# One pool of eight PSUM banks, a fourth output buffer, later loads on SyncE alone, and a new order for an attention and ELU-MLP kernel

## The chip, the cores and the metric

The kernel runs on one core of one Trainium2 chip. The metric is the device time of one execution in microseconds, as a median over runs. Engines: TensorE (PE) for matmuls, VectorE (DVE), ScalarE (ACT), GpSimd (POOL), and SyncE (SP), which only issues DMAs here; ScalarE and GpSimd issue some as well.

## The reference

Causal attention with 16 extra "beacon" keys and values that every query sees, over 8 batches and 8 heads of 576 tokens with 64 columns, and then a two-layer MLP with an ELU between, over all 4608 tokens.

```python
k_all = concatenate([beacon_k, k], axis=2)        # 16 + 576 keys
v_all = concatenate([beacon_v, v], axis=2)
scores = q @ k_all^T / 8, causal on the 576 own keys
a = exp(scores - max) / (sum + 1e-9)
x = (a @ v_all) reshaped to [B * S, H * D] = [4608, 512]
h = x @ w_in                                       # 512 -> 2048
out = where(h > 0, h, exp(min(h, 0)) - 1) @ w_out  # 2048 -> 512
```

All inputs and the output are float32.

## The kernel before

**The work.** A batch is taken as four pairs of heads (n = 4 * batch + pair). For batches 0 to 2 (below `PE_B`) queries and keys of a pair are loaded into an `st` buffer, cast into an `sb` buffer and transposed on TensorE (`do_T`, `do_T2`); from batch 3 on they are loaded by tokens (`load_tok`, `load_tok2`), cast (`cast_tok`) and transposed by SP as DMA transposes (`turn_tok`, line 446, ten for a batch). Values go through `vst` buffers (`load_v`, `cast_v`). Scores are computed in units (`do_SC`, line 504): the matmuls of a unit use 64 rows of TensorE for each of the two heads and fill two PSUM banks. ScalarE takes the exponential of a unit (`do_exp`, line 513) into an `et` buffer, GpSimd masks it (`do_mask`, line 518), TensorE multiplies with the values and a column of ones (`do_AV`, line 532), and VectorE divides (`do_norm`, lines 545 and 546). The result is transposed into `xT`, a ring of four batches: on TensorE for batches 0 and 1 (`do_xT`), and as DMA transposes on SP from batch 2 on (`turn_x`, line 552).

**The MLP** runs over eleven tiles of tokens (128, 128, 256, then 512 each). `do_mm1` (line 584) makes one bank of 512 columns from four matmuls; ScalarE takes its exponential (`do_e`, line 591), GpSimd clamps that (`do_clamp`, line 595), VectorE joins both into `gt` (`do_join`, line 602), and then the bank is free. `do_mm2` (line 626) adds up sixteen matmuls, in four steps, in one bank for 128 tokens; VectorE copies it to an `osb` buffer (`do_osb`, line 632) and SP stores it (`do_store`, line 636). A `fill` (line 334) is a matmul on a column of ones without use for the result; it keeps TensorE at work while it would wait.

**The order.** Nothing runs in the order in which it is written. `Program.add` gathers 1734 operations, each with the engines that may take it, what it depends on, and which buffers it takes and gives back. `Program.run` then goes through the list `ORDER` (numbers of operations; -k stands for k fills), with `PICKS` naming the engine of each operation that has a choice and `PLACES` the number of each buffer. Each engine runs its own operations in this order, and waits where an input or a buffer is not ready. The lists come from a planner that is not part of the kernel.

**PSUM** is eight banks of 512 float32. Before, four of them are single banks ("bank": `do_mm1`, `do_mm2`, `do_AV`, `do_xT`, `do_T2`, fills) and four form two pairs ("pair": `do_SC`, `do_T`). Three `osb` buffers, six `st` and six `vst` buffers are on hand. Loads may be issued by SP or by ScalarE ("SA"); 27 load operations are ScalarE's, eight of them for batch 0 and the rest spread up to batch 7.

Of the kernel before, what the change touches and what calls it, by code (L numbers as in the profile page):

```python
# [8 lines left out]
FP32 = mybir.dt.float32  # L9
# [4 lines left out]
P = 128  # L14

ORDER = [i for t in """
# [96 lines left out]
class Program:  # L113
# [7 lines left out]
    def run(self, order, picks, places, fill):  # L121
# [10 lines left out]
        for i in order:  # L132
# [5 lines left out]
            op = self.ops[i]  # L138
            assert not op.done and all(d.done for d in op.deps)
            got = []  # L140
            for room in op.take:
                at = int(next(places), 36)
                assert (room, at) not in used
                used.add((room, at))
                op.held.append((room, at))
                got.append(self.rooms[room][at])
# [743 lines left out]
```

## Time and profile before

| | |
|---|---|
| median of 3 runs | 350.59 us (349.97 to 351.15) |
| the profiled execution | 349.6 us, of which its span is 347.8 us |
| granted TensorE clock, mean | 0.999 |
| moved by DMA | 52.54 MB, 127664 of 140631 packets under 512 B |
| DMA engines' busy share | 0.7 to 0.9 in most slices up to 260 us, near 0 in several after that |

The profile is of one execution. Times are in microseconds from the start of the span; "PE bank L584 x8" is eight TensorE instructions of line 584 that write a tile named bank. Matmuls overlap, so the time between two starts, not the length of one, says what it costs. SPq and ACTq are the DMA-issuing instructions of SP and ScalarE. The waits give, for an engine that stood idle, what ended that; the chain follows the work that ended last back from the end.

### The profile page before, as it was taken

The page shows a single profiled execution, that of the slowest core. Times are in us where ns is not written, and L with a number is a line of the kernel's source. Part 1 is how long each engine was busy: PE and PEld are TensorE (multiplying, and loading weights), DVE is VectorE, ACT ScalarE, POOL GpSimd, SP SyncE. Part 2 cuts the span into 40 slices and gives each one's busy share as a digit, 9 for nine tenths or more (in the row PEclk, how much of TensorE's full clock was granted, in tenths as well). Part 3 has the DMA queues.
Part 4 walks back from the last instruction along what each step waited for, and adds up shares of the span by engine and source line. Part 5 has one row for each costly group of instructions (what it writes and reads, how often), then busy time and mean ns, then how long its engine had stood idle before and what let it go on. Part 6 is the DMA issues. An engine that isn't in the chain of part 4 may idle for free.

```text
span 347.8 us, 8391 instructions
## 1 busy us (share of the span) xinstructions
PE 337.6 (97%) x3300; PEld 192.2 (55%) x3300; DVE 184.0 (53%) x399; ACT 203.7 (59%) x296; POOL 190.3 (55%) x357
## 2 busy tenths in 40 slices
PE   7999999999998999999999999999999999999996
PEld 5667787454553555455466764456445554444444
DVE  4777685465541665366335552656255634744431
ACT  1786795678717891796477455886197504632300
POOL 2687897457545676566358643765085503642400
PEclk9999999999999999999999999999999999999999
DMA  7999999899799999997899699955740062000112
GB/s 211 236 243 237 188 221 228 200 268 153 161 211 142 191 208 175 186 177 170 142 224 218 136 190 210 158 96 121 122 111 2 5 181 76 0 14 18 60 61 92
DMA packets 140631, 52.54 MB, mean 151 GB/s; under 512 B 127664, under 2 KB 134064, under 8 KB 140592
## 3 DMA queue, kind: packets, MB, share of 16 engines
q1 hardware_dynamic: 115264, 41.78, 58.4%
q10 hardware_dynamic: 21104, 6.03, 8.7%
q0 software_dynamic: 4224, 4.19, 7.5%
q8 instruction: 26, 0.43, 0.6%
q14 instruction: 13, 0.11, 0.1%
HBM read 37.22 MB, written 9.44 MB: 134 GB/s over the span
## 4 chain that ended last, share of the span: by engine, by line
PE 86%; DMA 6%; DVE 2%; issue 1%; POOL 1%; SPq 1%; ACT 1%; ACTq 0%; POOLq 0%; DVEq 0%
PE bank L626 35%; PE bank L584 34%; PE bank L532 8%; PE pair L504 8%; DMA w_in<-in_moe_w_in_dram 3%; DMA out_dram<-osb 2%; DMA st<-in_q_dram 1%; PE pair L386 1%; PE bank L334 1%; SPq L365 1%; ACT et L513 1%; POOL et L518 0%; DVE x L546 0%; PE bank L561 0%; DVE sb L331 0%
## 5 line engine op out<-in xcount | busy, mean ns | idle before, releaser
L513 ACT ACTIVATE et<-pair 128x1024 f16<-128x1024 f32 (+3 forms) x113 | 103.5, 957 | 64.6 <-PE pair L504 60.1
L584 PE MATMUL bank<-xT,w_in 128*128 128x512 f16 (+2 forms) x768 | 134.9, 326 | 2.6 <-DMA w_in<-in_moe_w_in_dram 1.3
L626 PE MATMUL bank<-w_out,gt 128*128 128x512 f16 (+1 forms) x592 | 133.8, 373 | 0.0
L602 DVE SCALAR_TENSOR_TENSOR gt<-e,bank 128x512 f16<-128x512 f32 x144 | 95.9, 685 | 68.8 <-POOL e L595 67.9
L595 POOL TENSOR_SCALAR e<-e 128x512 f32<-128x512 f32 x144 | 87.3, 612 | 74.6 <-ACT e L591 73.3
L591 ACT ACTIVATE e<-bank 128x512 f32<-128x512 f32 x144 | 84.5, 604 | 57.9 <-PE bank L584 56.4
L584 PEld LDWEIGHTS <-w_in 128*128 128x128 f16 x768 | 66.9, 98 | 56.0 <-issue 4.2
L518 POOL TENSOR_SCALAR_AFFINE_SELECT et<-et 128x256 f16<-128x256 f16 (+3 forms) x145 | 59.1, 424 | 54.4 <-ACT et L513 54.1
L626 PEld LDWEIGHTS <-gt 128*128 128x128 f16 x592 | 55.4, 98 | 59.6 <-issue 1.3
L632 DVE COPY osb<-bank 128x512 f32<-128x512 f32 (+1 forms) x37 | 24.8, 674 | 55.9 <-PE bank L626 43.4
L532 PEld LDWEIGHTS <-et 128*128 128x128 f16 (+1 forms) x960 | 34.8, 97 | 8.4 <-issue 1.0
L532 PE MATMUL bank<-v,et 128*128 128x65 f16 (+1 forms) x960 | 37.2, 193 | 0.3 <-DVE x L546 0.3
L504 PE MATMUL pair<-qT,kT 64*128 64x80 bf16 (+4 forms) x744 | 35.3, 225 | 1.1 <-ACT et L513 1.1
L546 DVE TENSOR_TENSOR x<-bank,rl 128x256 f16<-128x256 f32 (+2 forms) x68 | 32.1, 472 | 2.3
L331 POOL CAST sb<-st 128x1024 bf16<-128x1024 f32 (+4 forms) x30 | 28.2, 940 | 8.0 <-DMA st<-in_q_dram 8.0
L504 PEld LDWEIGHTS <-kT 64*128 64x128 bf16 x744 | 20.9, 95 | 19.1 <-issue 15.6
L545 DVE RECIPROCAL rl<-bank 128x4 f32<-128x4 f32 (+2 forms) x68 | 12.4, 182 | 21.2 <-PE bank L532 20.7
L334 PE MATMUL bank<-ones 128*128 128x256 bf16 x76 | 14.4, 311 | 1.3 <-DVE ones L841 1.3
L331 POOL CAST v<-vst 128x512 f16<-128x512 f32 (+1 forms) x20 | 12.2, 617 | 3.2 <-DMA vst<-in_v_dram 2.0
L329 ACT ACTIVATE v<-vst 128x512 f16<-128x512 f32 (+1 forms) x19 | 11.4, 632 | 0.0
L334 PEld LDWEIGHTS <-ones 128*128 128x128 bf16 x76 | 7.6, 110 | 4.5 <-issue 1.4
L329 ACT ACTIVATE sb<-st 128x1024 bf16<-128x1024 f32 (+3 forms) x10 | 9.4, 948 | 0.0
(39 smaller groups left out, 68.7 us busy)
## 6 DMA issues: line engine op xcount, KB each, us to landing
out_dram<-osb SPq DMA_DIRECT2D x35, 256.0 KB, 2.7
vst<-in_v_dram SPq DMA_DIRECT2D x18, 256.0 KB, 4.6
st<-in_q_dram SPq DMA_DIRECT2D x15, 256.0 KB, 5.1
st<-in_k_dram SPq DMA_DIRECT2D x12, 256.0 KB, 4.5
st<-in_k_dram SPq DMA_DIRECT2D x8, 288.0 KB, 5.6
st<-in_q_dram SPq DMA_DIRECT2D x8, 288.0 KB, 7.1
w_in<-in_moe_w_in_dram POOLq DMA_DIRECT2D x4, 512.0 KB, 10.5
w_out<-in_moe_w_out_dram POOLq DMA_DIRECT2D x4, 512.0 KB, 9.1
```

The source lines that it names most:

```text
L331: e.tensor_copy(out=out, in_=in_)
L334: nc.tensor.matmul(out=bank[:, 0:2 * P], lhsT=ones[:, 0:P], rhs=ones, start=True, stop=True)
L504: e.matmul(out=pair[:, h, o:o + w], lhsT=kT[D * h:D * h + D, P * jc:P * jc + P], rhs=qT[D * h:D * h + D, q0:q0 + w], start=True, stop=True ...
L513: e.activation(out=et[:, :, 0:w], in_=scs[n, u][:, :, 0:w], func=AFT.Exp, bias=0.0, scale=float(1.0 / (D ** 0.5)))
L518: e.affine_select(out=part, in_=part, compare_op=ALU.is_ge, fill=fill0, base=q0 + NB - P * jc, pattern=[[0, 2], [0, times], [1, dw]], chan ...
L532: e.matmul(out=av[:, c:c + D + 1], lhsT=ets[tuple(unit)][0:m, h, col:col + P], rhs=v16s[b % 2][0:m, jc, 2 * hp + h, 0:D + 1], start=(jc == ...
L546: e.tensor_tensor(out=x16s[b % 2][:, blks[0]:blks[-1] + 1:step, P * hp:P * hp + P].rearrange("q i (h d) -> q i h d", d=D), in0=av[:, :, :, ...
L584: e.matmul(out=bank[:, o:o + z - a], lhsT=w_in16[:, cc, P * fc:P * fc + P], rhs=xTa[:, cc, a % RING:a % RING + z - a], start=(cc == 0), st ...
L591: e.activation(out=t, in_=hpss[p, i], func=AFT.Exp, bias=0.0, scale=1.0)
L595: e.tensor_scalar(out=t, in0=t, scalar1=1.0, scalar2=0.0, op0=ALU.min, op1=ALU.max)
L602: e.scalar_tensor_tensor(out=gts[p, i // 2][:, i % 2], in0=es[p, i], scalar=1.0, in1=hpss[p, i], op0=ALU.subtract, op1=ALU.max)
L626: e.matmul(out=opss[p, t4][:, cols], lhsT=gt_of(p, fc)[:, P * t4:P * (t4 + 1)], rhs=w_out16[:, fc, cols], start=(fc == 0), stop=(fc == NFC ...
```

## The change

All eight banks lie in four tiles of two banks. A "bank" is one half of such a tile, a "pair" is the whole, so that any single bank may be taken by any of the single-bank operations, and up to four pairs may be in use at once. The bookkeeping of `Program.run` counts a pair as its two banks. There is a fourth `osb` buffer. Values of batches from `PE_B` = 3 on and all token loads (`load_tok`, `load_tok2`) are issued by SP alone ("S"); the loads of batches 0 to 2 may still be ScalarE's. `ORDER`, `PICKS` and `PLACES` are new in whole, planned with SP's own pace. ScalarE now has 6 load operations (four for batch 0, two for batch 2); fills are 78 instead of 76.

```diff
             for room in op.take:
                 at = int(next(places), 36)
-                assert (room, at) not in used
-                used.add((room, at))
-                op.held.append((room, at))
+                held = [("bank", at), ("bank", at + 1)] if room == "pair" else [(room, at)]
+                assert not used.intersection(held) and not (room == "pair" and at % 2)
+                used.update(held)
+                op.held.append(held)
...
             for other, i in op.give:
-                used.remove(other.held[i])
+                assert used.issuperset(other.held[i])
+                used.difference_update(other.held[i])
...
+    pairs = [psum.tile([P, 2, 512], FP32, name=f"banks_{i}") for i in range(4)]
...
-        "osb": tiles(3, [P, DM], FP32, "osb"),
-        "bank": [psum.tile([P, 512], FP32, name=f"bank_{i}") for i in range(4)],
-        "pair": [psum.tile([P, 2, 512], FP32, name=f"pair_{i}") for i in range(2)],
+        "osb": tiles(4, [P, DM], FP32, "osb"),
+        "bank": [pairs[i // 2][:, i % 2] for i in range(8)],
+        "pair": [pairs[i // 2] for i in range(8)],
...
-            got = add("SA", load_v, b, jc, take=["vst"])
+            got = add("SA" if b < PE_B else "S", load_v, b, jc, take=["vst"])
...
-                st = add("SA", load_tok, b, is_k, c, take=["st"])
-                got = [st] + ([add("SA", load_tok2, b, is_k, c + 1, deps=[st])] if m == 2 else [])
+                st = add("S", load_tok, b, is_k, c, take=["st"])
+                got = [st] + ([add("S", load_tok2, b, is_k, c + 1, deps=[st])] if m == 2 else [])
...
```

The three lists `ORDER`, `PICKS` and `PLACES` are left out here.

More of the change, by code (lines that the diff above doesn't have):

```diff
@@ L16 @@
 ORDER = [i for t in """
[69 rows of a table removed]
[69 rows of a table added]
 """.split() for i in ([int(t)] if int(t) >= 0 else [-1] * -int(t))]
 PICKS = (
-    "GSVAGSGSGSGSAVVSSGVASVVSSVAAAVVAAGVASVVSSVVVVAVVVVVVAVAASASASASGSGSSGASSGVSSGVSSGVVVAVGSAAASAAASGSSGASSAASSGVS"
-    "SGVSGSGAASASGSSASSGSGSSASSGSGSGSAAGSGSGSSGSSGAGSSGASGSAAASGSGSASGASGSAGSAASASSASGSASAAASGAASAGSSASGASGSSGSGAAS"
-    "GSASASGAAGSSASASAGASGSG"
+    "GSVAGSGSASGSAVVSSVVASVVSSGVSSGVSSGVASVVSSVVVVAVAVVVAVAVASASASASGSGSSGASSGVSSGVSSGVAAVVGSGAGSGSGSGSSGASSGVSAAVS"
+    "SGVAAAGGGGGGGGGGGGAGGGAAGAGAGAGGAGGAAGGAAGGAAGGAGAAGGAAGGA"
@@ L91 @@
 )
 PLACES = (
-    "00101111111111111111111012213333333333212300233333333331101322222111003214215333306333033312011113127010003123"
-    "31105741135400120221121630203001123130120301231332451000111102323215070011112323300010121421522106223330001361"
-    "1452273050173310100132210563113100320301112323203042351201418041712950330A22101323B101120C2021001211D321320006"
-    "100033E0135431200211312F20010310012111014071120022101030152340000113025172021100312131G150320H1062131003043221"
-    "20704132214201503302110110623301310371223001204623120214013020311203421151701032110301252515060233E1F101405003"
@@ L98 @@
-    "202317001191203213201200322B033C101022D0110617300101210511230318A350212430135012230313H1221340043131G201230012"
-    "2100130201227301061137500031423111201231054204250711000021031221203160312103112039220132C1112236100107122303F1"
-    "2015015203031001B13123104202110031210321D3E0612102000133A0711052102301G31041511120301232012014011803H123211003"
-    "213600302001102147335122C112300322611130032211300322B1130900F1303211108222033213000G210E2301112132H00321130011"
-    "200111320"
+    "01001111111111111111111101111111131111223211114111106014220233034652222000000040627655542111111100323150622443"
@@ new lines @@
+    "33500020046471121615323423137603224536725505435521400655440216210100477732300131243516211324001252665124226337"
+    "037063220745304640207136254531646016345010467440672400153210465031207810292A304350B7610111323C04521202242501D2"
+    "432E16205053060143206003641F3765320420415603275250601244051037601321140251621004460672112634420260G7143H550601"
+    "421063711013422040321103327260160432511704203564512614060210655130324602113020264572064202400312135261E5127533"
+    "41F012B022426553423067044261D3012A251403C226074022003562140656732120891001021036011601252541431H71030246141322"
@@ L103 @@
+    "00230G5645316004212360543112270273607100034230112422041405641502032723301710B0012E405231225A502103721D23603122"
+    "7046076213165044262003124200132614025345043C12F61G730220314H10461007234230361526321104610473012242706451902071"
+    "464512033154736162801B7063242D2710021135E2305A20143601222737043521214201073423C21F15090011326G0274015013223411"
+    "70212170302"
 )
```

138 rows, old and new, of the table ORDER are left out of this document.

## The prediction

> **What bounds the kernel now.** I read the page first (span, busy shares, the chain that ended last), then the busy time by stretches, then the waits, and last the timeline around each place where TensorE stood still.
>
> ```profile
> span 347.8 us, 8391 instructions
> PE 337.6 (97%) x3300; PEld 192.2 (55%) x3300; DVE 184.0 (53%) x399; ACT 203.7 (59%) x296; POOL 190.3 (55%) x357
> PE 86%; DMA 6%; DVE 2%; issue 1%; POOL 1%; SPq 1%; ACT 1%; ACTq 0%; POOLq 0%; DVEq 0%
> ```
>
> TensorE is busy 97% of the span and is 86% of the chain; no other engine passes 59%. The only time to win is TensorE's own work and the 347.8 - 337.6 = 10.2 us in which it idles. The busy time by stretches (first column the window, then its length, then TensorE's busy time) says where those lie:
>
> ```profile
> 0.00:40.00 40.00, 35.33 (x492) 26.62 (x492) 26.48 (x94) 24.29 (x36) 26.47 (x55) 1.00 1.02 229
> 40.00:105.00 65.00, 64.98 (x744) 39.20 (x741) 39.16 (x83) 44.11 (x66) 42.93 (x80) 1.00 1.01 203
> 105.00:115.00 10.00, 8.74 (x79) 4.06 (x79) 2.55 (x5) 6.92 (x10) 5.10 (x10) 1.00 1.01 153
> 115.00:170.00 55.00, 55.00 (x590) 29.13 (x587) 31.95 (x65) 39.24 (x56) 36.02 (x68) 1.00 0.98 183
> 170.00:175.00 5.00, 3.91 (x42) 1.86 (x35) 0.00 (x0) 2.60 (x3) 0.80 (x2) 1.00 0.94 118
> 175.00:340.00 165.00, 165.00 (x1338) 87.86 (x1337) 82.39 (x150) 86.54 (x128) 79.02 (x144) 1.00 0.51 106
> 340.00:347.80 7.80, 4.67 (x38) 3.47 (x36) 1.45 (x3) 0.00 (x0) 0.00 (x0) 0.97 0.20 70
> ```
>
> Idle: 4.7 us in the start, 1.3 around 110, 1.1 around 173, 3.1 at the end, nothing elsewhere; the granted clock is 1.00 throughout. So an edit can gain in the middle only by ending those two stops (2.4 us) or by making TensorE's own instruction stream shorter.
>
> **The stream itself: changes between score and other matmuls.** The scores (L504) use 64 rows, all else in the middle of the kernel uses 128 (or 80). From the timeline of TensorE (start, length, what) and the chain:
>
> ```profile
> 158.59 1.03 PE L626 MATMUL bank<-w_out,gt 128*128 128x512 f16 x4
> 159.55 0.39 PE L504 MATMUL pair<-qT,kT 64*128 64x256 bf16 x4
> 159.88 0.54 PE L532 MATMUL bank<-v,et 128*128 128x65 f16 x12
> ...
> 120.72 0.61 PE L504 MATMUL pair<-qT,kT 64*128 64x256 bf16 x8
> 121.26 0.71 PE L532 MATMUL bank<-v,et 128*128 128x65 f16 x18
> ...
> 242.49 7.77 PE bank L626 x36
> ```
>
> A 512-column matmul in an unbroken stream takes 7.77 / 36 = 0.216 us. The four before the scores at 159.55 took 159.55 - 158.59 = 0.96 instead of 0.86: 0.10 to get into the scores. One score unit alone holds the stream for 159.88 - 159.55 = 0.33; two in a row take 121.26 - 120.72 = 0.54. The second costs 0.21, so 0.12 of the single one's 0.33 is the way out. Each stretch of scores thus costs about 0.21 us beyond its columns.
>
> Counting both order lists after the first do_mm1: before has 97 score units in 54 stretches (11 of one, 43 of two, two being all that two pairs hold); after has the same 97 in 41 (5 of one, 16 of two, 20 of three). 13 stretches fewer x 0.21 = 2.7 us off a stream that has no slack. No row shows a stretch of three. If its third unit costs the 0.21 of the second, the gain is 2.7; if it costs the 0.33 of a fresh one and its surroundings the same 0.10, it is nothing. I take 2.7, because the row of two is the nearest and the third unit changes neither rows nor engine. The Trainium skill, TensorEngine Tiling (Array Packing), Key Properties, says that changing the tiling mode drains TensorE, and going to another tile of the same mode does not; by that rule, too, a third unit would pay no drain, and no run here shows it yet.
>
> Other TensorE work is equal in count; fills, put where it would wait, go from 76 to 78.
>
> **The two stops.** Rows of the waits (waiter, what it waited for, us, times, longest) and of the chain around each stop:
>
> ```profile
> DVE osb L632 <- DMA out_dram<-osb: 12.5, 2, 7.3
> ACT et L513 <- DMA out_dram<-osb: 4.2, 1, 4.2
> PE bank L584 <- DMA w_in<-in_moe_w_in_dram: 1.3, 2, 0.8
> ```
>
> ```profile
> 109.13 0.64 SPq L446
> ...
> 109.86 2.39 DMA out_dram<-osb
> ...
> 112.38 0.70 DVE osb L632
> ...
> 113.12 1.02 PE bank L584 x4
> ```
>
> First stop: the store of an earlier output block stood behind key and query transposes on SP (L446) until 109.86, all three osb buffers were held, and VectorE's copy (L632), with the joins queued behind it, kept banks from TensorE. A fourth osb buffer moves that point one block back. I count 0.6 of the 1.2 us: the same SP queue gets longer (below).
>
> ```profile
> 167.57 4.37 DMA out_dram<-osb
> ...
> 171.96 0.34 ACTq L482
> ...
> 173.32 1.03 ACT et L513
> ...
> 174.39 0.41 PE pair L504 x12
> ```
>
> Second stop: a value load on ScalarE's queue (L482) waited 4.4 us until a store of SP had landed, and the exps behind it in ScalarE's order waited too; TensorE then lacked a free pair. After has no load on ScalarE past batch 2 (27 of its load calls become 6), so this cannot recur: 1.1 us. The skill's DMA: Bandwidth & Descriptors, Issuing engines are not separate DMA queues, speaks against this part: several issuers only save the sequencer's issue time, all run on the same DMA engines. By that rule alone the move would gain nothing and the sum would be 1.1 smaller; the row above differs, for the 4.4 us were a wait in ScalarE's order and the issue itself took 0.34.
>
> **What the move costs.** 21 load calls leave ScalarE, 17 of them after the start, and four of those carry a beacon load too: 21 issues. On SP:
>
> ```profile
> 151.22 0.58 SPq L435 DMA_DIRECT2D st<-in_q_dram  x1
> ...
> 55.97 0.62 SPq L363 DMA_DIRECT2D st<-in_q_dram  x1
> 60.87 1.30 SPq L446 DMA_TRANSPOSE kT<-sb  x1
> ...
> 223.94 0.65 SPq L435 DMA_DIRECT2D st<-in_q_dram  x1
> 230.08 0.37 SPq L636 DMA_DIRECT2D out_dram<-osb  x1
> ...
> 245.71 1.20 SPq L446 DMA_TRANSPOSE kT<-sb  x1
> ```
>
> 21 x 0.58 = 12.2 us more on SP between about 60 and 225 us. Two of its gaps alone, 56.6 to 60.9 and 224.6 to 230.1, hold 9.8. What is queued behind a late load on SP: the transposes of keys, queries and outputs and the stores; who waits: the casts, the scores, do_mm1, and the output copy. I take zero for it, covered by those gaps and by loads issued well ahead; without cover it is the first rival. The four calls moved in the start cost SP 4 x 0.6 = 2.4 us among the first loads; the w_in loads stand in the same order on POOL, the second two casts earlier. Bounds for the start: 1.3 us gained (both w_in waits gone) to 2.4 lost; I take nothing, as TensorE has the same number of fills ahead of do_mm1. The choice of engine changes for some fifteen copies and casts, on engines that idle over 40% of the time: nothing. The end, four output blocks of the last tile, is the same in both lists: nothing.
>
> **More banks.** A do_mm1 finds its bank freed by a longer way back in the list. TensorE idles for no other bank reason in before, so this earns nothing beyond the longer stretches.
>
> **Sum.** 2.7 + 0.6 + 1.1 = 4.4 us. The profiled execution took 349.6 us (1.8 around the span): 345.2. The median of the runs shown, 350.59, is 1.0 higher; against it, 350.6 - 4.4 = 346.2 us.
>
> **Rivals.** (1) SP becomes what TensorE waits for; slower. Place: the first scores of a batch, which need all ten transposes.
>
> ```profile
> kT<-sb SPq DMA_TRANSPOSE x25, 3.4
> 250.25 0.56 PE pair L504 x20
> ```
>
> The last transpose of batch 7, issued at 245.71 for 1.20 us and landing 3.4 later by the median, was there at 250.3, and the batch's scores began at 250.25: no lead at all. For it: whatever lateness SP carries into that place becomes TensorE idle time. Against it: the gaps above, and no stop there in before. If half of the 12.2 us gets through, 346.2 + 6.1 = 352.3; it ends slower than before once more than 4.4 + 1.1 = 5.5 get through; all of it gives 358.4. This is also where the DMA page's rule would lead. Chance 0.20.
>
> (2) The stretches of three give their gain back in banks; about no change. Rows for it: a bank of do_mm1 from matmul to join, and the exp.
>
> ```profile
> 162.75 2.60 PE bank L584 x12
> ...
> 165.42 0.61 ACT e L591
> ...
> 166.10 0.62 POOL e L595
> ...
> 166.75 0.70 DVE gt L602
> ...
> L513 ACT ACTIVATE et<-pair 128x1024 f16<-128x1024 f32 x77 | 76.5, 1026 | 50.9 <-PE pair L504 46.7 <-DMA out_dram<-osb 4.2
> ```
>
> Three units hold six of eight banks while their exps take 3 x 1.03 = 3.1 us. The third do_mm1 of that run began at 162.75 + 1.73 = 164.48 and its bank was free at 167.45, 3.0 later. With two banks, two do_mm1 (1.73 us) fit into 3.0: 1.3 us lost. In the list 3 of the 20 triples are followed by three do_mm1 (13 by do_mm2, which stays in one bank): 3 x 1.3 = 3.9, so 350.1. Against it: most triples have their cover. Chance 0.12.
>
> (3) The change does not do what it says: two banks cut from one pair tile are kept apart only as one tile, so a writer of the one waits for the reader of the other. One in four of 144 do_mm1 waiting 1 us would be 36 us: 382. No row speaks for it, none excludes it. Chance 0.03.
>
> **How the numbers follow.** The forecast has the remaining 0.65. Its own range is 343.8 (all of both stops and the w_in waits gone: 350.6 - 2.7 - 2.4 - 1.3 = 344.2, and 0.4 for the run) to 348.6 (the start's 2.4 lost). For 8 in 10 I reach over rival 2 to the middle of rival 1: 343.8 to 352.5, which leaves out rival 3, the upper half of rival 1 and a few in a hundred below. Under 0.3% (1.1 us) this kernel's runs tell nothing. Faster: 0.65 and a little of rival 2, 0.66; same: 0.12, most of rival 2 with the edge of the first; slower: 0.22.
>
> **What would show it.** Right: pieces of L504 near 0.75 us in the chain (0.54 + 0.21); about 41 entries into scores; no load on ScalarE's queue after 100 us; no row of ACT et waiting for a store; TensorE idle below 1 us in all between 40 and 340. Wrong in the first step: stretches of three at 0.87. Rival 1 shows as TensorE idle behind L446, L552 or a load, most likely at the first scores of a batch; rival 2 as idle of L584 or L504 behind ACT et, DVE gt or POOL e within 3 us of a triple; rival 3 as that all over. A start that is over 1 us longer at the first do_mm2 would put the loss in SP's first loads. The forecast is wrong if stops of over 3.3 us in all (4.4 - 1.1) appear that before did not have.

## The result, and the profile after

The changed kernel takes 478.89 us (median of four runs, 477.74 to 479.18) where the kernel before takes 350.28 beside it: ratio 1.366 (95% interval 1.362 to 1.370), 128.6 us slower. The forecast was 346.2. The profiled execution took 477.74 us, of which its span is 475.9. The page of the changed kernel: span, busy shares, TensorE's busy time and granted clock in 40 slices, and the chain that ended last.

```profile
span 475.9 us, 8423 instructions
PE 369.9 (78%) x3302; PEld 207.9 (44%) x3302; DVE 183.2 (38%) x398; ACT 202.9 (43%) x294; POOL 193.0 (41%) x360
PE   5776776797879655897889588877798788769977
PEclk9998787999998967599999999989999999999979
PE 56%; DVE 15%; ACT 9%; POOL 7%; issue 6%; SPq 3%; DMA 3%; ACTq 0%; DVEq 0%; POOLq 0%
```

TensorE idles 475.9 - 369.9 = 106.0 us instead of 10.2, and is busy 369.9 us instead of 337.6 with the same work but for two more fills: 95.8 and 32.3 make up the 128.1 us of span. The loss is not in one place: 33 of the 40 slices are busy for less than nine tenths, where before has three. No other engine has become the bound: VectorE is busy for 183.2 us against 184.0 before, ScalarE 202.9 against 203.7, GpSimd 193.0 against 190.3, each under 44% of the span. By stretches (window, length, TensorE's busy time first), the start has 11.6 us of idle time instead of 4.7, and the middle 91:

```profile
0.00:40.00 40.00, 28.41 (x384) 21.37 (x384) 19.72 (x83) 17.14 (x24) 17.89 (x40) 1.00 0.99 238
40.00:460.00 420.00, 328.87 (x2853) 179.51 (x2848) 160.53 (x310) 185.77 (x271) 175.07 (x320) 0.93 0.48 99
```

The waits of the changed kernel (waiter, what it waited for, us, times, longest) name the place:

```profile
PE banks L586 <- DVE gt L604: 34.5, 19, 3.3
ACT e L593 <- DVE gt L604: 23.9, 14, 4.9
PE banks L586 <- ACT e L593: 19.6, 15, 3.4
DVE gt L604 <- PE banks L586: 15.0, 3, 9.8
PE banks L628 <- DVE gt L604: 10.2, 8, 2.7
```

None of these five pairs has a row among the waits of before. The first could be a bank that comes free late. The fourth could not: a join (L604) reads a bank whose exponential and clamp are done, so its own four matmuls ended long ago, and still it waits for a do_mm1 (L586), up to 9.8 us. That must be a do_mm1 in another bank, which the experiments below put to the test. All rows of TensorE waiting with a `banks` tile come to 84 waits and 102.2 us; before has 11 and 6.9 with its `bank` and `pair` tiles. TensorE's timeline in a stretch that is all MLP (start, length, what; in brackets the idle time before it and what ended that), and then the chain of waits in it, show what that makes of the pipeline (the last row of the timeline is cut by the window's end):

```profile
399.82 2.75 PE L586 MATMUL banks<-xT,w_in 128*128 128x512 f16 x12 [0.73 <-ACT e L593]
403.74 1.02 PE L586 MATMUL banks<-xT,w_in 128*128 128x512 f16 x4 [1.17 <-DVE gt L604]
405.45 0.81 PE L586 MATMUL banks<-xT,w_in 128*128 128x512 f16 x3 [0.69 <-ACT e L593]
```

```profile
401.68 0.61 ACT e L593
...
402.35 0.62 POOL e L597
...
403.00 0.70 DVE gt L604
...
403.74 1.04 PE banks L586 x4
...
404.80 0.61 ACT e L593
...
405.45 1.04 PE banks L586 x4
```

After three do_mm1 TensorE stands for 1.17 us until an exponential, a clamp and a join have gone through one behind the other; after one more it stands for 0.69 us until an exponential ends, a reader that frees no bank: a bank comes free with its join. In the kernel before the same line ran fifteen do_mm1 without a break, 0.86 us each:

```profile
291.97 12.95 PE bank L584 x60
```

### The profile page after: what moved, and what is told of

It reads as the page before. It is cut to its first block, busy times and chain, and to the rows that moved or that the text cites. A ratio compares the mean times of both kernels' runs of the same rounds, so it can differ in the third digit from the quotient of the medians.

```text
span 475.9 us, 8423 instructions
## 1 busy us (share of the span) xinstructions
PE 369.9 (78%) x3302; PEld 207.9 (44%) x3302; DVE 183.2 (38%) x398; ACT 202.9 (43%) x294; POOL 193.0 (41%) x360
## 4 chain that ended last, share of the span: by engine, by line
PE 56%; DVE 15%; ACT 9%; POOL 7%; issue 6%; SPq 3%; DMA 3%; ACTq 0%; DVEq 0%; POOLq 0%
PE banks L628 25%; PE banks L586 20%; DVE gt L604 7%; ACT e L593 6%; PE banks L534 6%; POOL e L597 5%; DVE x L548 4%; PE banks L506 3%; ACT et L515 3%; DMA st<-in_q_dram 2%; DVE rl L547 1%; DVE osb L634 1%; POOL sb L333 1%; DMA st<-in_k_dram 1%; SPq L367 1%
## 5 line engine op out<-in xcount | busy, mean ns | idle before, releaser
L586 PE MATMUL banks<-xT,w_in 128*128 128x512 f16 (+2 forms) x768 | 150.4, 350 | 59.6 <-DVE gt L604 34.5
L628 PE MATMUL banks<-w_out,gt 128*128 128x512 f16 (+1 forms) x592 | 139.6, 382 | 18.4 <-DVE gt L604 10.2
L593 ACT ACTIVATE e<-banks 128x512 f32<-128x512 f32 x144 | 82.9, 597 | 155.2 <-PE banks L586 104.0
L604 DVE SCALAR_TENSOR_TENSOR gt<-e,banks 128x512 f16<-128x512 f32 x144 | 94.1, 683 | 130.6 <-POOL e L597 97.5
L515 ACT ACTIVATE et<-banks 128x1024 f16<-128x1024 f32 (+3 forms) x113 | 101.8, 956 | 87.9 <-PE banks L506 84.4
L586 PEld LDWEIGHTS <-w_in 128*128 128x128 f16 x768 | 75.2, 106 | 125.5 <-issue 78.5
L634 DVE COPY osb<-banks 128x512 f32<-128x512 f32 (+1 forms) x37 | 25.0, 675 | 68.4 <-PE banks L628 60.8
L534 PE MATMUL banks<-v,et 128*128 128x65 f16 (+1 forms) x960 | 39.7, 199 | 11.5 <-DVE x L548 3.8
L506 PE MATMUL banks<-qT,kT 64*128 64x80 bf16 (+4 forms) x744 | 34.1, 231 | 1.2 <-DVE qT L333 1.0
L548 DVE TENSOR_TENSOR x<-banks,rl 128x256 f16<-128x256 f32 (+2 forms) x68 | 32.0, 471 | 2.3
L333 POOL CAST sb<-st 128x1024 bf16<-128x1024 f32 (+5 forms) x31 | 29.7, 961 | 4.3 <-DMA st<-in_q_dram 4.3
L331 ACT ACTIVATE v<-vst 128x512 f16<-128x512 f32 (+1 forms) x17 | 10.2, 625 | 0.0
```

The lines of the kernel that those rows point to most:

```text
L333: e.tensor_copy(out=out, in_=in_)
L506: e.matmul(out=pair[:, h, o:o + w], lhsT=kT[D * h:D * h + D, P * jc:P * jc + P], rhs=qT[D * h:D * h + D, q0:q0 + w], start=True, stop=True ...
L515: e.activation(out=et[:, :, 0:w], in_=scs[n, u][:, :, 0:w], func=AFT.Exp, bias=0.0, scale=float(1.0 / (D ** 0.5)))
L534: e.matmul(out=av[:, c:c + D + 1], lhsT=ets[tuple(unit)][0:m, h, col:col + P], rhs=v16s[b % 2][0:m, jc, 2 * hp + h, 0:D + 1], start=(jc == ...
L548: e.tensor_tensor(out=x16s[b % 2][:, blks[0]:blks[-1] + 1:step, P * hp:P * hp + P].rearrange("q i (h d) -> q i h d", d=D), in0=av[:, :, :, ...
L586: e.matmul(out=bank[:, o:o + z - a], lhsT=w_in16[:, cc, P * fc:P * fc + P], rhs=xTa[:, cc, a % RING:a % RING + z - a], start=(cc == 0), st ...
```

## The experiments

Two theories for it. **The tie**: two banks cut from one tile are guarded as one, so the program itself contains the waits. **The order**: the new lists plan for a chip that the real one isn't, late loads on SP or too few free banks (rivals 1 and 2 of the prediction). And for the gain that did not show: **covered** (the forecast's sum holds underneath) or **not**. All kernels here compute the whole reference.

### Ties without the new order: e1 and e6

```diff
-"bank": [psum.tile([P, 512], FP32, name=f"bank_{i}") for i in range(4)],
+ties = [psum.tile([P, 2, 512], FP32, name=f"tie_{i}") for i in range(2)]
+"bank": [ties[i // 2][:, i % 2] for i in range(4)],                                              # e1
+"bank": [tie[:, 0], tie[:, 1]] + [psum.tile([P, 512], FP32, name=f"bank_{i}") for i in (2, 3)],  # e6
```

> The kernel before, with its four single banks cut from two tiles of two banks; order, buffers, loads and number of banks are as before. Theory (tie): two banks of one tile are guarded as one, so an instruction on one bank waits for the users of the other; then this alone must cost tens of microseconds, 380 us or more, with TensorE's do_mm1 waiting for do_join and do_e, and ScalarE's do_e for do_join. Rivals (the longer SP queue, the new order with its stretches of three score units, the fourth output buffer): none of them is in this kernel, so it stays at 350.

> The kernel before with banks 0 and 1 cut from one tile, banks 2 and 3 single. Theory (a tile is guarded as one): between 350 (no tie) and 518 (both tied); if the waits of the two ties add up, near 434, and rather above half the way, since the banks of a pair of do_mm1 are taken in turn. Rival (the loss comes with the two-bank shape of all singles, not with each tie): 350 or 518.

Measured: e1 518.35 us, ratio 1.477 (1.464 to 1.491); e6 444.78, ratio 1.270 (1.265 to 1.275). The order, the loads and the osb buffers are those of before; only the cut of four PSUM banks differs. One tie costs 94.6 us, two cost 168. The waits of e1, its chain and TensorE's timeline:

```profile
PE tie L585 <- DVE gt L603: 67.8, 41, 2.9
DVE gt L603 <- PE tie L627: 6.9, 5, 3.1
```

```profile
442.09 1.04 PE tie L585 x4
...
443.15 0.61 ACT e L592
...
443.83 0.62 POOL e L596
...
444.48 0.70 DVE gt L603
...
445.22 1.04 PE tie L585 x4
```

```profile
442.09 2.01 PE L585 MATMUL tie<-xT,w_in 128*128 128x512 f16 x8 [1.16 <-DVE gt L603]
445.22 2.01 PE L585 MATMUL tie<-xT,w_in 128*128 128x512 f16 x8 [1.12 <-DVE gt L603]
```

The chain is a loop with no overlap left: matmuls, exponential, clamp, join, and only then the next matmuls, 445.22 - 442.09 = 3.13 us. In each round TensorE does eight matmuls, two do_mm1, and stands 1.12 us until a join ends. Four banks behave like two: 1.57 us for a do_mm1 instead of 0.86. The tie alone does more than the whole slowdown of the change. One tie already brings 94.6 / 168.5 = 56% of the price of two, so the prices of ties don't simply add up.

### The new order without ties: e2 and e8, with e4 as its control

```diff
-    pairs = [psum.tile([P, 2, 512], FP32, name=f"banks_{i}") for i in range(4)]
+    singles = [psum.tile([P, 512], FP32, name=f"bank_{i}") for i in range(8)]
-        "bank": [pairs[i // 2][:, i % 2] for i in range(8)],
-        "pair": [pairs[i // 2] for i in range(8)],
+        "bank": singles,
+        "pair": [singles[i // 2 * 2:i // 2 * 2 + 2] for i in range(8)],
...
-            out=et[:, :, 0:w], in_=scs[n, u][:, :, 0:w], func=AFT.Exp, bias=0.0, scale=float(1.0 / (D ** 0.5)))
+        for h in range(2):
+                out=et[:, h, 0:w], in_=scs[n, u][h][:, 0:w], func=AFT.Exp, bias=0.0, scale=float(1.0 / (D ** 0.5)))
```

An instruction cannot reach over two tiles, so every exponential of a unit becomes two, and the copies out of `do_T` are split as well. e4 is before with these splits and its own order; e8 is e2 again beside e7.

> The changed kernel with eight single-bank tiles: a pair is two tiles, each exp is two instructions of one bank, and the copies after do_T are split at the bank's edge. Order, picks, places, loads and output buffers are those of the changed kernel. Theory (tie): the 128 us go, and it comes to 345 to 358, the forecast of 346 plus up to 12 us for 113 more ScalarE instructions. Rivals (SP queue, order, stretches of three): it stays above 450, since all of them are still in it.

> A control for the second run: the kernel before with each pair as two single-bank tiles and each exp as two instructions, nothing else. All theories: 350 to 358; it prices the splitting, which the run without ties pays too.

> The changed kernel with eight single tiles and split exps once more, with more rounds and beside the run with ScalarE's loads. It should be 345 to 348 again, 1 to 1.5% below the kernel before.

Measured: e2 346.55 us, ratio 0.987 (0.979 to 0.994); e8 346.19, ratio 0.988 (0.986 to 0.991); e4 351.44, ratio 1.005 (1.002 to 1.008). Order, engines, osb buffers and the banks' numbers are those of the changed kernel, and 132 us are gone: the order theory falls, and so does any conflict between neighbouring banks. TensorE's busy line of e2 and then of e4:

```profile
PE 336.0 (97%) x3302; PEld 194.5 (56%) x3302; DVE 182.1 (53%) x412; ACT 209.4 (61%) x409; POOL 191.8 (55%) x360
```

```profile
PE 338.9 (97%) x3300; PEld 192.7 (55%) x3300; DVE 185.7 (53%) x412; ACT 210.5 (60%) x412; POOL 190.5 (54%) x357
```

With the splits in both, the new order takes 338.9 - 336.0 = 2.9 us off TensorE's stream. The chain of e2 shows the stretches of three, and its stretches the two stops of before:

```profile
102.91 0.78 PE bank L511 x26
103.69 2.70 PE bank L634 x12
106.39 0.77 PE bank L511 x22
```

```profile
105.00:115.00 10.00, 10.00 (x81) 4.66 (x80) 2.30 (x4) 9.91 (x20) 7.03 (x16) 1.00 0.95 179
170.00:175.00 5.00, 5.00 (x51) 2.38 (x50) 0.69 (x1) 4.15 (x10) 1.54 (x5) 1.00 0.67 95
```

Three units hold the stream for 0.77 to 0.78 us, where two took 0.54. TensorE is busy all of both windows.

### The loads on SP by themselves: e3 and e7

e3 is before with 17 letters of PICKS changed (the ScalarE loads of batches 3 to 7 go to SP, at the same places in ORDER). e7 is e2 with the same 17 given back to ScalarE.

```diff
-            got = add("SA" if b < PE_B else "S", load_v, b, jc, take=["vst"])
+            got = add("SA", load_v, b, jc, take=["vst"])                         # e7, load_tok and load_tok2 alike
```

> The kernel before with its 17 load calls of ScalarE for batches 3 to 7 issued by SP, nothing else changed. Theory (tie): 348 to 356; the stop at 173 us, where ScalarE's load held the exps, goes, and SP carries some 12 us more. Rival (SP is what the changed kernel waits for): 400 or more.

> The changed order without ties (as in the run of the changed kernel with eight single tiles), but the 17 load calls of batches 3 to 7 that ScalarE issued before are ScalarE's again. It prices moving the loads under the new order. If SP's own pace is covered there (the forecast's zero) and ScalarE's loads hold the exps as at 173 us of before, it is 1 to 4 us slower than with the loads on SP: 347 to 351. If SP's 12 us are what TensorE waits for, it is faster by 1 us or more: 345 or less.

Measured: e3 355.47 us, ratio 1.013 (1.007 to 1.019), 5.6 us slower than before; e7 353.79, ratio 1.009 (1.006 to 1.012), 7.6 slower than e8 beside it. The same move costs 5.6 us under the old order and is worth 7.6 under the new. The stretches and waits of e3, then the stretches, waits and a piece of the chain of e7:

```profile
105.00:115.00 10.00, 7.25 (x66) 3.26 (x64) 0.56 (x1) 6.10 (x8) 4.88 (x10) 1.00 0.65 133
...
DVE osb L632 <- DMA out_dram<-osb: 15.1, 3, 9.7
...
PE bank L584 <- DVE osb L632: 4.2, 2, 3.8
```

```profile
115.00:170.00 55.00, 51.02 (x524) 27.73 (x522) 28.20 (x59) 35.84 (x68) 34.30 (x63) 0.97 0.96 168
...
175.00:340.00 165.00, 162.09 (x1333) 86.46 (x1332) 79.14 (x149) 90.24 (x169) 77.06 (x142) 1.00 0.53 107
```

```profile
DVE osb L641 <- DMA out_dram<-osb: 18.2, 3, 8.1
...
PE bank L593 <- DVE osb L641: 3.9, 1, 3.9
```

```profile
139.99 5.81 DMA out_dram<-osb
```

In e3 the first stop of before has grown from 1.2 to one of 3.8 us, from 112.2 to 116.0: VectorE's copy waits 9.7 us for an output store, and TensorE for the copy. SP issues that store at 111.89 where before did at 109.86, and two of the moved loads now stand ahead of it. So SP comes late to what is queued on it, not at the first scores of a batch, where rival 1 looked for it, but at the output store. The second stop of before is gone in e3: from 117 to 340 us TensorE has no stop over 0.5 us.

In e7 there are 4.0 us of idle time between 115 and 170 where e2 has 0.8, nearly all of it in one stop of 3.9 us that ends at 146.66. It is of the same kind, though there are four osb buffers: the copy waits for a store that is issued at 139.99 and lands 5.8 us later, against a median of 2.6 in this run. The expectation had looked for 1 to 4 us, with exponentials held behind ScalarE's loads; it was 7.6, and no exponential of a score unit waits for a DMA in e7. ScalarE issues four loads beside that store, from 138.38 on, but what made it late was not tried, nor whether it is that each list was planned for its own issuers.

### How large a tile is tied: e5, e9, e10 and e11

The tie theory in its plain form says that a larger tile is worse.

```diff
-    pairs = [psum.tile([P, 2, 512], FP32, name=f"banks_{i}") for i in range(4)]
+    whole = psum.tile([P, 8, 512], FP32, name="whole")                          # e5, e10
+    pairs = [whole[:, 2 * i:2 * i + 2] for i in range(4)]
+    wholes = [psum.tile([P, 4, 512], FP32, name=f"whole_{i}") for i in range(2)]   # e9
+    pairs = [wholes[i // 2][:, 2 * (i % 2):2 * (i % 2) + 2] for i in range(4)]
```

e11 is before with its four banks and two pairs cut from one tile of eight, in the same places.

> The changed kernel with all eight banks cut from one tile instead of four. Theory (a tile is guarded as one): every user of PSUM waits for every other, so it gets far worse than 479, 700 us or more. Rival (only the same bank is guarded, and the banks are slow side by side on the chip): the banks lie where they lay, so it stays at 479.

> The changed kernel with its eight banks cut from two tiles of four banks. The theory that any tile is guarded as one fell with the one tile of eight (347.6). What remains: a tile of fewer than all eight banks is guarded as one, a tile of all eight bank by bank. Then four tied banks are worse than two: above 479, some 550 to 700. Rival (larger tiles are guarded more finely): between 348 and 479.

> The changed kernel with one tile of all eight banks once more, now timed in rounds, as the version that may beat both: exps whole, no ties. The run with eight single tiles and split exps took 346.2, and splitting costs 1.6 in the kernel before; so 344.5 to 347, 1 to 1.6% below the kernel before.

> A control: the kernel before with its four single banks and two pairs cut from one tile of eight banks, all else as before. If the tile of eight only keeps the banks apart and brings nothing by itself, it stays within 0.5% of 350. If the shape itself is a gain or a loss, it moves by more.

Measured: e5, all eight banks in one tile, 347.64 us in one run. The plain form had fallen, and with it the rival that left it at 479. The mended one, that tiles of two or four banks are guarded as one and a tile of all eight is not, was then put to e9, e10 and e11. e9: 713.17 us, ratio 2.032 (2.020 to 2.044): above 479, as the mended form has it, and a little above the 550 to 700 that was expected. e10, which is e5 timed: 346.60, ratio 0.988 (0.984 to 0.992). e11: 350.95, ratio 1.000 (0.998 to 1.003). Lines of e9's page, then of e10's:

```profile
span 714.0 us, 8438 instructions
PE 465.4 (65%) x3302; PEld 242.0 (34%) x3302; DVE 185.7 (26%) x398; ACT 207.6 (29%) x294; POOL 193.6 (27%) x360
```

```profile
span 342.8 us, 8409 instructions
PE 335.3 (98%) x3302; PEld 193.7 (56%) x3302; DVE 180.6 (53%) x398; ACT 202.4 (59%) x294; POOL 192.3 (56%) x360
```

The order of the changed kernel, by tiles: eight of one bank 346.2 to 346.6, four of two 478.9, two of four 713.2, one of eight 346.6. The waits of e10 that are left of the five rows of after:

```profile
ACT e L594 <- DVE gt L605: 8.2, 13, 1.6
```

The same kind of wait, 6.6 us in all, is there in e2 without any shared tile, so it is not the tie's. In the instruction lists that these kernels compile to, the semaphore waits stand already: of the 144 joins (the wait may stand in the join or in a waiting instruction just ahead of it), none waits for TensorE in before, 16 in after, 13 in e1, 8 in e6, 31 in e9, 2 in e2 and e10. So the waits are put in when the program is built. Why a tile of eight is followed bank by bank, and smaller ones not, the runs don't show; it is an observation.

**e10 beats both kernels**: it is the changed kernel with its banks cut from one tile of eight, two lines other, and takes 0.988 of the time before.

## Why the prediction was wrong

**Rival 3 was the case, and was mis-sized twice.** Its mechanism, "two banks cut from one pair tile are kept apart only as one tile, so a writer of the one waits for the reader of the other", is what e1, e2 and e6 show. What failed in it are its chance, 0.03, and its price, 36 us for "one in four of 144 do_mm1 waiting 1 us". Measured are 39 waits before do_mm1's matmuls, so the one in four was close, but 1.5 us each (59.5 us); 45 more before other matmuls, 18.2 us of them for do_mm2 and 11.4 for do_AV, which take banks of the same pool (102.2 us in all); and then 32.3 us more busy time for the same matmuls, of which the price had nothing. The price was also one-sided. Readers wait too: ScalarE's exponential for the join of the other bank (23.9 us, of which e10 keeps 8.2 without a tie), the join for the other bank's matmuls (15.0).

**The term "More banks" was costed at nothing without a row for it, and this is the step that failed.** The measured cost of that edit is the whole loss: 478.9 us with the four tiles of two banks, 346.2 to 346.6 without their ties. The prediction asked what more banks would bring, and not what cutting them from shared tiles costs. Before could not show it, as a pair there is written and read as one by design. "No row speaks for it, none excludes it" was true. But then the bound for that edit was the loop without overlap, whose parts were in the quoted rows: 1.02 + 0.61 + 0.62 + 0.70, about 3 us. One do_mm1 at a time in it would be 144 x 2.1, some 300 us; two at a time, as in e1, 144 x 0.7, some 100. (These hold for the full clock: e9, with a mean granted clock of 0.775, lost 363.) That end was not worked out, and not even the 382 was an end of the range.

**The sum of 4.4 us held underneath.** With the ties gone, in spans: one tile of eight, (342.8 + 345.7) / 2 = 344.3 of e10 and e5 against 348.6 for before and e11, 4.3 less; single tiles, 345.25 of e2 and e8 against e4's 350.0, 4.75 less. By medians e10 stands 4.4 below e11. The forecast of 346.2 is e10's 346.6 and e8's 346.2. That the total fits this closely is luck in part, as its terms are not measured as finely:

- *Stretches of scores, 2.7 us.* e2 against e4 2.9; over all profiles (e2 and e8 336.0 and 333.9 against 338.9; e5 and e10 336.3 and 335.3 against 337.6 and 338.0) between 1.3 and 5.0. "Pieces of L504 near 0.75": 0.77 to 0.78. The third unit costs 0.23 to 0.24, so the choice between 0.21 and the price of a fresh stretch was right.
- *The two stops, 0.6 and 1.1 us.* Both are gone in e2, the first in whole and not by half. The move of the loads ends the second by itself (e3). But idle time fell by 0.8 us (single tiles, mean of two) to 2.3 (one tile), as some came elsewhere. What the fourth osb alone brings was not tried; e7 has four and still a stop at the output copy.
- *SP's 12.2 us at zero, and rival 1.* Right as taken, and right as rival, each under its order: under the new order the move is covered, under the old it is not. So the move and the order were not terms to be added, as the prediction added them: without the move the new order is 3.6 us slower than before (e7, 1.6 of which is what splitting cost in e4), without the new order the move is 5.6 slower (e3).
- *Rival 2.* Did not appear: in e10 all waits of matmuls for anything but a DMA come to 3.7 us, the start's among them.

**The check by profile was right.** "Rival 3 as that all over" is what the page shows: idle time in 33 of 40 slices, behind DVE gt and ACT e. Of the signs for the forecast, seen where the ties are gone, one is missed: TensorE idles 1.9 us between 40 and 340 in e10 and 2.5 in e2, not below 1. The others hold: 41 stretches of scores, ScalarE's last load at 70 and 72 us, and no exponential that waits for a store. (Its "the granted clock is 1.00 throughout" passes over the 0.97 in the last row that it quotes, from the end of before, where the last matmul is done; nothing rests on it.)

## What to carry to other kernels

A tile is a unit of bookkeeping as well as of space: when banks with separate users are cut from one tile, look in the compiled instructions or in the waits for one user waiting for the other's. An engine that waits for an instruction whose result it doesn't read is the sign (here a join waiting for the do_mm1 of another bank). And an edit for which no row of the profile has a price, but which all of the work passes through, gets the loop without overlap as its bound, whatever its chance.

## What the runs showed of the hardware

**Stops cost twice.** TensorE's 32.3 us of added busy time come with a lower granted clock: the mean is 0.939 in the profiled run of after, 0.929 in e1, 0.973 in e6, 0.775 in e9, and 0.99 to 1.00 where banks are not tied. Windows of after (the third number from the end of a row is the granted clock), TensorE's timeline in the second of them, and pieces of the chain:

```profile
51.17:54.58 3.41, 1.25 (x12) 0.97 (x11) 1.45 (x3) 1.19 (x2) 1.43 (x3) 1.00 0.00 0
54.58:57.99 3.41, 3.41 (x24) 2.82 (x24) 0.72 (x2) 0.60 (x1) 0.85 (x2) 0.50 0.02 5
...
168.00:180.00 12.00, 6.42 (x35) 2.68 (x32) 4.79 (x11) 4.21 (x8) 3.04 (x5) 0.61 0.48 78
...
456.60:472.60 16.00, 16.00 (x80) 8.20 (x79) 2.50 (x4) 0.00 (x0) 0.00 (x0) 0.87 0.21 75
```

```profile
54.56 3.57 PE L586 MATMUL banks<-xT,w_in 128*128 128x128 f16 x24 [2.16 <-DVE gt L604]
```

```profile
171.31 1.87 PE banks L586 x4
...
175.82 3.58 PE banks L586 x8
...
456.58 16.08 PE banks L628 x80
```

Four matmuls of do_mm1 take 1.87 us here and 1.04 at 403.74. The last eighty matmuls, an unbroken stream in both kernels, take 16.08 us where before took 13.87 for the same work. In these traces the granted clock is either 1.0 or 0.5, in stretches of 3.41 us or multiples of it. The first two rows show a drop: in 3.41 us TensorE was busy for 1.25, with one stop of 2.16, and for the next 3.41 us it had half the clock, though it was busy all the time. The nine drops of after within its work all follow 3.41 us in which TensorE was busy for 0.37 to 1.37.

The Trainium skill, TensorE: Matmul & The Clock Gate, Part 1, says that TensorE's clock falls to half after an idle window of about 3.4 us and comes back after as long a busy one. The half and the length agree with the trace. But the window need not be idle throughout: here the longest single wait of a matmul was 3.4 us and the mean 102.2 / 84 = 1.2, and a window with a stop of 2.16 us was enough.

TensorE is busy for 47.5 us in the stretches at half clock; if that doubles their time, it makes 23.8 of the 32.3 us, by estimate. The rest, 8.5 us, is 0.10 for each of the 84 waits, and need not be the clock: a do_mm1 that stands alone is busy for 1.04 us at full clock, one in a stream costs 0.86. This was read from the records, and not tried by itself.
